# An attention and two expert layers in one kernel: the values' transfers issued as their buffer frees, shifted copies made head by head, the rests of q and k loaded by pairs of heads, and the first two batches of scores side by side

## The chip, the cores and the metric

The kernel runs on one core of a Trainium2 chip. The metric is the device time of one execution in microseconds (us), as the median of three runs.

## The reference

Only the first part, the attention, is touched by the change. What it feeds is told in one sentence each.

```python
def _attn_ref(q, k, v):
    B, H, S, D = q.shape          # 4, 8, 576, 64, float32
    window, dilation = 32, 4
    scores = np.matmul(q, k.transpose(0, 1, 3, 2)) / np.sqrt(D)
    rel = pos[:, None] - pos[None, :]
    mask_plain = (rel >= 0) & (rel < window)
    mask_dil = (rel >= 0) & (rel < window * dilation) & (rel % dilation == 0)
    # heads 0 to 3 use mask_plain, heads 4 to 7 mask_dil
    attn = softmax(np.where(mask, scores, -1e9))
    return np.matmul(attn, v)
```

The result, as 2304 rows of 512, goes through a soft mixture of experts (8 experts of 4 slots, weights moe_w1 and moe_w2, 33.5 MB in float32) and then through a second layer (h = x @ w_in, g = h - tanh(h), g @ w_out, weights of 64-bit elements, 16.8 MB), which gives the output of 2304 x 512.

## The kernel before

The attention is cut into 16 units. A unit is one head h of a pair of batch entries (`units`, each with h and the pair's number pr); the two entries lie on partitions 0 to 63 and 64 to 127 and are called ab or a in the code. Units 0 to 7 have the plain window ("nat" in the code), units 8 to 15 the dilated one. A unit has 9 blocks of 64 queries, and each block sees at most 96 keys. Four blocks at a time form a batch (`batches`, 38 of them; a dilated unit's last block counts twice). For each batch, TensorE (PE) makes scores (`scores`, tile sc, L401), DVE adds the mask and takes the maximum off (sm, L405 and L409), PE transposes (`flip`, tile pp, L420), ScalarE (ACT) takes the exponential (pT, L421), PE multiplies with the values (`mix`, tile pv, L431), and DVE divides (`norm`). The loop over k_ (from -2) does the scores of batch k_, the flip of batch k_ - 1 and the mix of batch k_ - 2, and between them takes up to three pieces off the list `extras` (`pick`). Such a piece is a `turn`: the transpose of a unit's q, k or rest on PE (tiles tr_q, tr_k, tr_e) and the copy to qT or kT on ACT.

q and k arrive in three tiles for a unit: "q" and "k" with the first 512 rows, and "e" with the rest, rows 512 to 575 of both. The transfers land in tiles that GpSimd (POOL) puts in another order (`regroup`, L279); unit 0's are loaded in that order at once. The values of a pair of units (two heads of the same pair of entries) go into one of two tiles vw, by turns: partitions 32 to 95 are filled by transfers (`load_v`), and partitions 0 to 31 hold the last 32 keys of the block before, copied from partitions 64 to 95 of the tile by POOL (`shift_v`, L301). For dilated units four more copies follow (L305), and a pair takes ten transfers instead of four. A tile of values is free when the mix of the last batch of the two units before has been done, which is what at stands for in the loop.

All transfers are issued by SyncE (SP), in program order; SP waits until the tile is free, and until one of eight semaphores in rotation is free, so at most eight are under way. Once an iteration one of the 24 first weight tiles of the experts is issued too (`w_load`, L229). In the first iterations PE also does matmuls whose result is not used (`stir`, tile warm; before them tile idle, L482). The vector phi is loaded in iteration 2 (L535) and scaled by POOL in iteration 3 (L538).

After the attention come the dispatch, the experts and the second layer. Their code is not changed. They run on the same engines, with a planner that fixes the second layer's order.

## Time and profile before

| | us |
|---|---|
| median of three runs (343.49 to 345.18) | 344.07 |
| the profiled execution | 346.59 |
| its span | 344.8 |
| PE busy | 309.5 |
| DVE busy | 223.5 |
| ACT busy | 163.8 |
| POOL busy | 108.6 |

The profile is of one execution, and all rows below are of it. PE's busy time holds matmuls at either of its two clocks. An engine's idle time matters where PE waits for it. The attention ends near 136 us of the span.

### The profile page before, as it was taken

The page shows a single profiled execution, that of the slowest core. Times are in us where ns is not written, and L with a number is a line of the kernel's source. Part 1 is how long each engine was busy: PE and PEld are TensorE (multiplying, and loading weights), DVE is VectorE, ACT ScalarE, POOL GpSimd, SP SyncE. Part 2 cuts the span into 40 slices and gives each one's busy share as a digit, 9 for nine tenths or more (in the row PEclk, how much of TensorE's full clock was granted, in tenths as well). Part 3 has the DMA queues.
Part 4 walks back from the last instruction along what each step waited for, and adds up shares of the span by engine and source line. Part 5 has one row for each costly group of instructions (what it writes and reads, how often), then busy time and mean ns, then how long its engine had stood idle before and what let it go on. Part 6 is the DMA issues. An engine that isn't in the chain of part 4 may idle for free.

```text
span 344.8 us, 7801 instructions
## 1 busy us (share of the span) xinstructions
PE 309.5 (90%) x2867; PEld 223.4 (65%) x2867; DVE 223.5 (65%) x744; ACT 163.8 (48%) x304; POOL 108.6 (31%) x195
## 2 busy tenths in 40 slices
PE   8977999988999998999999378879999999999990
PEld 5766887867788785643434256657765787787670
DVE  2355586773788686446315759868775678977591
ACT  2345455532373644322204367527784656655431
POOL 0354233205343110015003889966990000000000
PEclk9999699996999999999999789969999999999997
DMA  5877999596778898879999999573000013302003
GB/s 130 235 211 242 277 291 309 159 259 188 205 207 247 243 364 303 309 266 377 413 403 374 378 340 313 161 252 125 2 1 0 3 64 119 122 2 89 33 3 130
DMA packets 57885, 70.22 MB, mean 204 GB/s; under 512 B 29040, under 2 KB 45296, under 8 KB 57840
## 3 DMA queue, kind: packets, MB, share of 16 engines
q1 hardware_dynamic: 57840, 69.65, 62.7%
q8 instruction: 25, 0.41, 0.5%
q14 instruction: 20, 0.16, 0.2%
HBM read 64.91 MB, written 4.72 MB: 202 GB/s over the span
## 4 chain that ended last, share of the span: by engine, by line
PE 42%; POOL 7%; DVE 5%; issue 3%; ACT 2%; ACTq 0%; DVEq 0%; POOLq 0%
PE acc L1014 17%; PE h L1039 4%; PE h L1038 4%; PE hp L712 3%; PE sop L727 3%; POOL X L804 3%; PE ht L719 2%; DVE r L1050 2%; POOL X L801 1%; PE sp L634 1%; PE p L907 1%; PE msum L981 1%; ACT u L1043 1%; PE dt L607 1%; PE sit L626 1%
## 5 line engine op out<-in xcount | busy, mean ns | idle before, releaser
L1014 PE MATMUL acc<-whi,r 128*128 128x512 f32 x288 | 80.0, 398 | 1.8 <-DVE r L1050 1.1
L1043 ACT ACTIVATE u<-h,co 128x512 f32<-128x512 f32 (+1 forms) x80 | 51.0, 648 | 44.7 <-PE h L1039 36.8
L1050 DVE SCALAR_TENSOR_TENSOR r<-h,co,u 128x512 fp32r<-128x512 f32 (+1 forms) x80 | 55.0, 695 | 25.5 <-PE acc L1014 18.1
L1014 PEld LDWEIGHTS acc<-whi,r 128*128 128x128 f32 x288 | 52.5, 188 | 16.5 <-issue 2.4
L405 DVE CUSTOM_DVE_ANT_0 sm<-sc,m_sb 128x96 f32<-128x96 f32 x144 | 29.3, 259 | 11.4 <-PE sc L401 11.1
L401 PE MATMUL sc<-kT,qT 64*64 64x96 f32 (+1 forms) x608 | 35.8, 260 | 0.0
L431 PE MATMUL pv<-vw,pT 96*64 96x65 f32 x608 | 28.1, 234 | 6.9 <-POOL vw L301 4.3
L421 ACT ACTIVATE pT<-pp 96x512 f32<-96x512 f32 x38 | 23.1, 607 | 22.8 <-PE pp L420 22.8
L431 PEld LDWEIGHTS pv<-vw,pT 96*64 96x64 f32 x608 | 22.3, 143 | 15.2 <-issue 6.8
L1039 PE MATMUL h<-cT,Gs 128*128 128x512 f32 (+1 forms) x80 | 30.3, 385 | 0.9 <-DVE r L1050 0.7
L401 PEld LDWEIGHTS sc<-kT,qT 64*64 64x64 f32 x608 | 28.2, 139 | 4.3 <-issue 1.5
L339 ACT COPY qT<-tr_q 128x512 f32<-128x512 f32 x16 | 13.6, 848 | 25.8 <-PE tr_q L329 25.8
L420 PE MATMUL pp<-c_sb,sm 128*96 128x128 f32 x152 | 24.4, 285 | 0.0
L279 POOL TENSOR_SCALAR qm<-q 128x512 f32<-128x512 f32 x15 | 9.6, 641 | 42.3 <-PE tr_q L329 20.5
L409 DVE TENSOR_TENSOR sm<-sm,mx 128x384 f32<-128x384 f32 (+1 forms) x38 | 22.0, 580 | 1.2
L437 DVE TENSOR_SCALAR rd<-pv 128x4 f32<-128x4 f32 (+1 forms) x38 | 6.1, 159 | 25.4 <-PE pv L431 25.4
L301 POOL TENSOR_SCALAR vw<-vw 32x1024 f32<-32x1024 f32 (+1 forms) x16 | 13.2, 824 | 29.1 <-DMA vw<-in_v 27.4
L355 ACT COPY xT<-xt 128x512 f32<-128x512 f32 (+1 forms) x19 | 14.5, 784 | 12.4 <-PE xt L346 11.4
L1038 PE MATMUL h<-cT 128*128 128x512 f32 x64 | 20.2, 440 | 0.0
L1039 PEld LDWEIGHTS h<-cT,Gs 128*128 128x128 f32 x80 | 15.3, 191 | 5.7 <-DVE r L1050 2.2
L420 PEld LDWEIGHTS pp<-c_sb,sm 128*96 128x96 f32 x152 | 17.0, 130 | 3.0 <-issue 1.4
L804 POOL TENSOR_SCALAR X<-raw_i 128x512 bf16<-128x512 int16 x16 | 14.1, 908 | 11.4 <-DMA raw_i<-in_moe_w_in 10.9
(205 smaller groups left out, 524.1 us busy)
## 6 DMA issues: line engine op xcount, KB each, us to landing
w<-in_moe_w SPq DMA_DIRECT2D x60, 512.0 KB, 6.9
raw_o<-in_moe_w_out SPq DMA_DIRECT2D x16, 512.0 KB, 7.8
raw_i<-in_moe_w_in SPq DMA_DIRECT2D x15, 512.0 KB, 9.4
q<-in_q SPq DMA_DIRECT2D x15, 256.0 KB, 3.8
k<-in_k SPq DMA_DIRECT2D x15, 256.0 KB, 3.9
out<-X SPq DMA_DIRECT2D x14, 256.0 KB, 2.4
vw<-in_v SPq DMA_DIRECT2D x16, 144.0 KB, 3.6
vw<-in_v SPq DMA_DIRECT2D x32, 64.0 KB, 3.9
```

The costliest lines, as they stand in the source:

```text
L401: nc.tensor.matmul(dst[half, lo:hi], lhsT=qT[u % NQ][half, i:i + QB], rhs=keys[half], start=True, stop=True)
L405: nc.vector.tensor_tensor_reduce(out=sm[:, o:o + n, :].rearrange("p g k -> p (g k)"), in0=sc[:, o:o + n, :].rearrange("p g k -> p (g k)"), ...
L409: nc.vector.tensor_tensor(out=sm[:, o:o + n], in0=sm[:, o:o + n], in1=mx[:, o:o + n].unsqueeze(2).to_broadcast([128, n, KB]), op=ALU.subtract)
L420: nc.tensor.transpose(pp[:, i, :], sm[:, i, :], ident)
L421: nc.scalar.activation(out=pT, in_=pp, func=AF.Exp, scale=0.125)
L431: nc.tensor.matmul(pv[64 * ab:64 * ab + 64, i, :], lhsT=pT[:, o + x, 64 * ab:64 * ab + 64], rhs=w[:, ab, u % 2, j + x, :], start=x == 0, s ...
L804: nc.gpsimd.tensor_scalar(out=half(piece, 1, BF16), in0=quarter(piece, 3, I16), scalar1=2.0, scalar2=-2.0, op0=ALU.min, op1=ALU.max)
L1014: nc.tensor.matmul(live[key], lhsT=lhsT(), rhs=rhs(), start=new, stop=stop)
L1038: nc.tensor.matmul(live["h", key], lhsT=cT[:, 0:128], rhs=cT[:, c0:c0 + w], start=True, stop=True)
L1039: nc.tensor.matmul(live["h", key], lhsT=Gs[:, 128 * f:128 * (f + 1)], rhs=cT[:, c0:c0 + w], start=True, stop=True)
L1043: nc.scalar.activation(out=live["u", key], in_=live["h", key], func=AF.Square, scale=co[:, SC, f:f + 1])
L1050: nc.vector.scalar_tensor_tensor(out=live["r", key], in0=live["h", key], scalar=co[:, BB, f:f + 1], in1=live["u", key], op0=ALU.add, op1=A ...
```

## The change

- The values: `load_v` goes head by head, and within a head first batch entry 0, then 1; the rests come last. The transfers of units 2 and 3 are issued ahead of the loop; later pairs issue five transfers in each of two iterations, from the one in which the tile comes free, instead of three in each of four.
- The shifted copies: for the first pair ahead of the loop (before: in iterations 1 and 2); for later pairs head 0 in the third and head 1 in the fourth iteration after the tile comes free (before: both heads together, in the fifth at the latest).
- The rests "e" of q and k: one tile for two units, filled by four transfers, issued with the odd unit's turn. The first of them goes through ACT's queue.
- Unit 0's q and k: one transfer each, put in order by DVE.
- Iteration 0 stops after its scores and stirs, so that the scores of batches 0 and 1 follow each other; what was picked in it is picked in iteration 1.

```diff
@@ -251,47 +251,45 @@
             qT = [pools[i].tile([128, S], F32, name=f"qT{i}") for i in range(NQ)]
             kT = [pools[i].tile([128, 32 + S], F32, name=f"kT{i}") for i in range(NQ)]
             vw = [pools[i].tile([KB, 2, 2, NB + 1, D + 1], F32, name=f"vw{i}") for i in range(2)]
-            NR = 3
             raws, ms = {}, {}
 
-            def load_qk(u, nm):
+            def load_qk(u, nm, eng=nc.sync):
                 h, pr = units[u]
                 at = slice(2 * pr, 2 * pr + 2)
                 if nm == "e":
-                    t = raw.tile([128, 2, D], F32, tag=nm, name=f"{nm}_{u}", bufs=NR)
+                    t = raw.tile([128, 2, 2, D], F32, tag=nm, name=f"{nm}_{u}", bufs=2)
                     for x, src in enumerate((q, k)):
-                        nc.sync.dma_start(t[64 * x:64 * x + 64], src[at, h, 512:S].rearrange("a p d -> p a d"))
+                        for a in range(2):
+                            eng.dma_start(t[64 * x:64 * x + 64, :, a], src[2 * pr + a, h:h + 2, 512:S].rearrange("h p d -> p h d"))
+                    raws[u, nm], raws[u + 1, nm] = t[:, 0], t[:, 1]
                 else:
-                    src = q if nm == "q" else k
-                    if u == 0:
-                        t = raw.tile([128, 4, 2, D], F32, tag=nm + "m", name=f"{nm}m_{u}", bufs=2)
-                        for a in range(2):
-                            nc.sync.dma_start(t[:, :, a], src[2 * pr + a, h, 0:512].rearrange("(p r) d -> p r d", r=4))
-                        ms[u, nm] = t
-                        return
-                    t = raw.tile([128, 2, 4 * D], F32, tag=nm, name=f"{nm}_{u}", bufs=2)
-                    nc.sync.dma_start(t, src[at, h, 0:512].rearrange("a (p r) d -> p a (r d)", r=4))
-                raws[u, nm] = t
+                    t = raws[u, nm] = raw.tile([128, 2, 4 * D], F32, tag=nm, name=f"{nm}_{u}", bufs=2)
+                    eng.dma_start(t, (q if nm == "q" else k)[at, h, 0:512].rearrange("a (p r) d -> p a (r d)", r=4))
 
             def regroup(u, nm):
                 t = raws.pop((u, nm))
                 ms[u, nm] = raw.tile([128, 4, 2, D], F32, tag=nm + "m", name=f"{nm}m_{u}", bufs=2)
-                nc.gpsimd.tensor_scalar(out=ms[u, nm].rearrange("p r a d -> p a r d"), in0=t.rearrange("p a (r d) -> p a r d", r=4), scalar1=1.0, scalar2=0.0, op0=ALU.mult, op1=ALU.add)
+                dst, src = ms[u, nm].rearrange("p r a d -> p a r d"), t.rearrange("p a (r d) -> p a r d", r=4)
+                if u == 0:
+                    nc.vector.tensor_copy(dst, src)
+                else:
+                    nc.gpsimd.tensor_scalar(out=dst, in0=src, scalar1=1.0, scalar2=0.0, op0=ALU.mult, op1=ALU.add)
 
             def load_v(u):
                 h, pr = units[u]
                 w = vw[u // 2 % 2]
-                for ab in range(2):
-                    vb = v[2 * pr + ab, h:h + 2]
-                    if h < H // 2:
-                        for h2 in range(2):
-                            yield nc.sync.dma_start(w[32:96, ab, h2, 0:NB, 0:D], vb[h2].rearrange("(j p) d -> p j d", p=64))
-                        continue
-                    vi = vb.rearrange("h (i r) d -> h r i d", r=4)
-                    for h2 in range(2):
-                        for x in (1, 0):
-                            yield nc.sync.dma_start(w[32:96, ab, h2, 4 * x:4 * x + 4, 0:D], vi[h2, :, 64 * x:64 * (x + 1)].rearrange("r i d -> i r d"))
-                    yield nc.sync.dma_start(w[32:96, ab, :, 9, 0:D], vb[:, 512:576].rearrange("h p d -> p h d"))
+                nat = h < H // 2
+                for h2 in range(2):
+                    for ab in range(2):
+                        vb = v[2 * pr + ab, h + h2]
+                        if nat:
+                            yield nc.sync.dma_start(w[32:96, ab, h2, 0:NB, 0:D], vb.rearrange("(j p) d -> p j d", p=64))
+                            continue
+                        for x in range(2):
+                            yield nc.sync.dma_start(w[32:96, ab, h2, 4 * x:4 * x + 4, 0:D], vb[256 * x:256 * (x + 1)].rearrange("(i r) d -> i r d", r=4))
+                if not nat:
+                    for ab in range(2):
+                        yield nc.sync.dma_start(w[32:96, ab, :, 9, 0:D], v[2 * pr + ab, h:h + 2, 512:576].rearrange("h p d -> p h d"))
 
             def shift_v(u, parts=(0, 1)):
                 w = vw[u // 2 % 2]
@@ -299,7 +297,7 @@
                 for h2 in parts:
                     dst, src = (slice(1, NB), slice(0, NB - 1)) if nat else (slice(4, 8), slice(0, 4))
                     nc.gpsimd.tensor_scalar(out=w[0:32, :, h2, dst, 0:D], in0=w[64:96, :, h2, src, 0:D], scalar1=1.0, scalar2=0.0, op0=ALU.mult, op1=ALU.add)
-                if not nat:
+                if not nat and 1 in parts:
                     for r in range(4):
                         p = 32 * (r % 3)
                         nc.gpsimd.tensor_scalar(out=w[p:p + 32, :, :, 8 + r // 3, 0:D], in0=w[64:96, :, :, 4 + r, 0:D], scalar1=1.0, scalar2=0.0, op0=ALU.mult, op1=ALU.add)
@@ -468,10 +466,11 @@
                         regroup(u + 2, nm)
                         if u + 4 < NU:
                             load_qk(u + 4, nm)
-                    if nm == "e" and u + NR < NU:
-                        load_qk(u + NR, nm)
+                    if nm == "e" and u % 2 and u + 3 < NU:
+                        load_qk(u + 3, nm)
                 return done
 
+            load_qk(0, "e", nc.scalar)
             load_qk(0, "q")
             nc.sync.dma_start(c_sb[:, 0:128], cst[:, 0:128])
             load_qk(0, "k")
@@ -485,17 +484,21 @@
                     nc.vector.memset(kT[i][:, 0:32], 0.0)
                 nc.vector.memset(vw[i][:, :, :, :, D:D + 1], 1.0)
                 nc.vector.memset(vw[i][0:32, :, :, 0, 0:D], 0.0)
-            load_qk(0, "e")
-            for nm in "qke":
+            for nm in "qk":
+                regroup(0, nm)
+            for nm in "qk":
                 load_qk(1, nm)
-            for nm in "qk":
                 regroup(1, nm)
-            for _ in load_v(0):
-                pass
-            for nm in "qke":
-                load_qk(2, nm)
+            vloads = {u: load_v(u) for u in range(0, NU, 2)}
+            for u in (0, 2):
+                for _ in vloads[u]:
+                    pass
+                for nm in "qk" if u == 0 else "":
+                    load_qk(2, nm)
+            shift_v(0)
             for nm in "qk":
                 load_qk(3, nm)
+            load_qk(2, "e")
             warm = ps.tile([128, GB, D + 1], F32, tag="pv", name="warm").rearrange("p g d -> p (g d)")
 
             def stir(n):
@@ -503,10 +506,6 @@
                     nc.tensor.matmul(warm, lhsT=ident, rhs=m_sb[:, 0:GB * (D + 1)], start=True, stop=True)
 
             for k_ in range(-2, NBAT + 1):
-                if k_ == 1:
-                    shift_v(0, (0,))
-                if k_ == 2:
-                    shift_v(0, (1,))
                 if k_ >= 2 and len(w_sb) < min(WR, (k_ - 1) * WR // 31):
                     w_load(wright)
                 if k_ < 0:
@@ -519,6 +518,8 @@
                     scores(k_)
                 if k_ < 2:
                     stir(2)
+                if k_ == 0:
+                    continue
                 pick(k_)()
                 if k_ < 2:
                     stir(1)
@@ -548,15 +549,11 @@
                         w_load(early)
                 for u in range(2, NU, 2):
                     at = last[u - 3] + 2 if u > 2 else 0
-                    if k_ == at:
-                        vloads = load_v(u)
-                    if at <= k_ < at + 4:
-                        for _ in range(3):
-                            next(vloads, None)
-                    if k_ == min(at + 4, first[u] + 1):
-                        for _ in vloads:
+                    if at <= k_ < at + 2:
+                        for _, _ in zip(range(5), vloads[u]):
                             pass
-                        shift_v(u)
+                    if at + 2 <= k_ < at + 4:
+                        shift_v(u, (k_ - at - 2,))
             assert not extras
             mix(NBAT - 1)
             done0 = x_part(3, 1, 0)
```

Where this moves instructions. Names carry the unit's or the batch's number first (tr_q_1 is the transpose of unit 1's q, sc_1 the scores of batch 1). First PE from the scores of batch 0 to those of batch 2, before and now:

```order
L401 MATMUL sc_0_185<-kT0_101,qT0_99 64x96 x8
L503 MATMUL warm_153<-m_sb_92,c_sb_58 128x260 x2
L329 MATMUL tr_q_1_203<-c_sb_58,qm_1_134 128x128 x4
L503 MATMUL warm_153<-m_sb_92,c_sb_58 128x260
L329 MATMUL tr_k_1_214<-c_sb_58,km_1_136 128x128 x4
L317 MATMUL tr_e_1_224<-c_sb_58,e_1_131 128x128
L401 MATMUL sc_1_235<-kT0_101,qT0_99 64x96 x8
L503 MATMUL warm_153<-m_sb_92,c_sb_58 128x260 x3
L420 MATMUL pp_0_254<-c_sb_58,sm_0_186 96x128 x4
L401 MATMUL sc_2_263<-kT0_101,qT0_99 64x96 x2
```

```order
L399 MATMUL sc_0_191<-kT0_101,qT0_99 64x96 x8
L506 MATMUL warm_162<-m_sb_92,c_sb_58 128x260 x2
L399 MATMUL sc_1_209<-kT0_101,qT0_99 64x96 x8
L506 MATMUL warm_162<-m_sb_92,c_sb_58 128x260 x2
L327 MATMUL tr_q_1_227<-c_sb_58,qm_1_133 128x128 x4
L506 MATMUL warm_162<-m_sb_92,c_sb_58 128x260
L418 MATMUL pp_0_238<-c_sb_58,sm_0_192 96x128 x4
L327 MATMUL tr_k_1_245<-c_sb_58,km_1_137 128x128 x4
L315 MATMUL tr_e_1_255<-c_sb_58,e_0_105 128x128
L399 MATMUL sc_2_264<-kT0_101,qT0_99 64x96 x2
```

The scores of batch 1 have moved ahead of unit 1's three transposes, the flip of batch 0 has moved between them, and one stir is gone.

Second POOL from unit 3's regroups to unit 5's, before and now (vw0 holds the values of units 0 and 1, vw1 those of 2 and 3):

```order
L279 TENSOR_SCALAR qm_3_208<-q_3_149 128x2x4x64
L279 TENSOR_SCALAR km_3_219<-k_3_151 128x2x4x64
L301 TENSOR_SCALAR vw0_103<-vw0_103 32x2x8x64 x2
L279 TENSOR_SCALAR qm_4_284<-q_4_161 128x2x4x64
L279 TENSOR_SCALAR km_4_301<-k_4_171 128x2x4x64
L538 TENSOR_SCALAR phi_sb_59<-phi_sb_59 128x128
L279 TENSOR_SCALAR qm_5_390<-q_5_210 128x2x4x64
L279 TENSOR_SCALAR km_5_407<-k_5_221 128x2x4x64
L301 TENSOR_SCALAR vw1_104<-vw1_104 32x2x8x64 x2
```

```order
L276 TENSOR_SCALAR qm_3_232<-q_3_153 128x2x4x64
L276 TENSOR_SCALAR km_3_250<-k_3_155 128x2x4x64
L276 TENSOR_SCALAR qm_4_285<-q_4_170 128x2x4x64
L276 TENSOR_SCALAR km_4_302<-k_4_180 128x2x4x64
L299 TENSOR_SCALAR vw1_104<-vw1_104 32x2x8x64
L539 TENSOR_SCALAR phi_sb_59<-phi_sb_59 128x128
L299 TENSOR_SCALAR vw1_104<-vw1_104 32x2x8x64
L276 TENSOR_SCALAR qm_5_390<-q_5_234 128x2x4x64
```

Before, both heads of vw1 were shifted behind phi and unit 5's regroups. Now head 0 stands ahead of phi and head 1 right behind it; vw0's shift (not in these rows any more) now stands ahead of unit 2's regroups.

Third SP around the values of units 8 and 9 (vw0), before and now:

```order
L293 DMA vw0_103<-in_v 64x4x64 x3
L229 DMA w_10_1041<-in_moe_w1 128x1024
L293 DMA vw0_103<-in_v 64x4x64
L294 DMA vw0_103<-in_v 64x2x64
L293 DMA vw0_103<-in_v 64x4x64
L229 DMA w_11_1094<-in_moe_w1 128x1024
L273 DMA q_13_1119<-in_q 128x2x256
L273 DMA k_13_1136<-in_k 128x2x256
L263 DMA e_12_1155<-in_q 64x2x64
L263 DMA e_12_1155<-in_k 64x2x64
L293 DMA vw0_103<-in_v 64x4x64 x3
L229 DMA w_12_1163<-in_moe_w2 128x1024
```

```order
L267 DMA q_12_995<-in_q 128x2x256
L267 DMA k_12_1012<-in_k 128x2x256
L289 DMA vw0_103<-in_v 64x4x64 x5
L229 DMA w_10_1038<-in_moe_w1 128x1024
L289 DMA vw0_103<-in_v 64x4x64 x3
L292 DMA vw0_103<-in_v 64x2x64 x2
L229 DMA w_11_1093<-in_moe_w1 128x1024
L267 DMA q_13_1118<-in_q 128x2x256
```

The ten transfers of vw0 have only one weight between them now; before there were three weights, unit 13's q and k and unit 12's two rests. Before, the first five of these rows' transfers are entry 0's, and what unit 8's first four blocks read of entry 1 is the first of the last group of three; the tenth transfer comes behind one more weight.

## Rows read from the trace of the kernel before

**Rows 1.** Waits of PE from 0 to 136 us: total us, times, longest us.

```profile
PE pv L431 <- POOL vw L301: 4.3, 2, 2.3
PE pv L431 <- DMA vw<-in_v: 2.5, 1, 2.5
```

**Rows 2.** Timeline: start us, us, engine, instructions [idle before <- its end].

```profile
20.77 0.57 PE L431 MATMUL pv<-vw,pT 96*64 96x65 f32 x12 [2.26 <-POOL vw L301]
...
21.27 0.33 PE L317 MATMUL tr_e<-c_sb,e 128*128 128x128 f32 x1
```

**Rows 3.** Timeline around phi and the shift of unit 2.

```profile
22.50 0.62 POOL L279 TENSOR_SCALAR km<-k 128x512 f32<-128x512 f32 x1
...
26.64 0.59 SPq L535 DMA_DIRECT2D phi_sb<-in_moe_phi  x1
...
30.55 0.64 POOL L538 TENSOR_SCALAR phi_sb<-phi_sb 128x128 f32<-128x128 f32 x1 [7.42 <-DMA phi_sb<-in_moe_phi]
...
32.44 2.15 POOL L301 TENSOR_SCALAR vw<-vw 32x1024 f32<-32x1024 f32 x2
...
33.53 0.49 PE L431 MATMUL pv<-vw,pT 96*64 96x65 f32 x4 [2.02 <-POOL vw L301]
```

**Rows 4.** Timeline around the first values of unit 8.

```profile
65.03 2.51 SPq L293 DMA_DIRECT2D vw<-in_v  x3
...
73.19 1.90 SPq L293 DMA_DIRECT2D vw<-in_v  x3
...
78.45 1.13 PE L431 MATMUL pv<-vw,pT 96*64 96x65 f32 x14 [2.48 <-DMA vw<-in_v]
```

**Rows 5.** Stretches: busy us of PE, PEld, DVE, ACT, POOL; clock, DMA share, GB/s.

```profile
33.46:40.29 6.83, 6.76 (x57) 5.70 (x59) 2.64 (x16) 2.09 (x5) 2.26 (x4) 0.50 0.94 290
40.29:47.12 6.83, 6.83 (x115) 5.61 (x111) 5.73 (x35) 3.71 (x7) 3.32 (x4) 1.00 0.98 281
77.84:84.66 6.82, 6.21 (x53) 5.26 (x55) 2.12 (x12) 1.91 (x5) 4.38 (x8) 0.50 0.64 178
```

**Rows 6.** Timeline of the start.

```profile
9.34 0.88 PE L401 MATMUL sc<-kT,qT 64*64 64x96 f32 x16
...
12.64 1.12 ACT L339 COPY kT<-tr_k 128x512 f32<-128x512 f32 x1
...
13.96 1.58 PE L503 MATMUL warm<-m_sb,c_sb 128*128 128x260 f32 x6
...
15.91 0.88 PE L401 MATMUL sc<-kT,qT 64*64 64x96 f32 x16
...
16.02 0.59 ACT L421 ACTIVATE pT<-pp 96x512 f32<-96x512 f32 x1 [2.14 <-PE pp L420]
...
16.79 0.41 SPq L273 DMA_DIRECT2D k<-in_k  x1
```

**Rows 7.** The page's costliest groups and its DMA issues (last: us to landing).

```profile
L279 POOL TENSOR_SCALAR qm<-q 128x512 f32<-128x512 f32 x15 | 9.6, 641 | 42.3 <-PE tr_q L329 20.5
...
e<-in_q SPq DMA_DIRECT2D x16, 32.0 KB, 3.6
```

**Rows 8.** Long stretches, columns as in rows 5.

```profile
0.00:30.00 30.00, 25.89 (x265) 19.81 (x266) 13.59 (x79) 12.00 (x21) 7.59 (x15) 1.00 0.73 190
30.00:62.00 32.00, 29.86 (x402) 24.24 (x400) 20.82 (x118) 16.59 (x31) 13.35 (x18) 0.89 0.98 291
62.00:136.00 74.00, 71.15 (x1022) 56.60 (x1020) 52.36 (x283) 34.97 (x70) 19.72 (x41) 0.95 0.80 239
...
155.00:180.00 25.00, 24.42 (x213) 10.13 (x215) 10.00 (x24) 5.27 (x10) 6.09 (x12) 1.00 1.02 399
```

**Rows 9.** Timeline: the first shift for unit 4, its first product.

```profile
43.88 1.04 POOL L301 TENSOR_SCALAR vw<-vw 32x1024 f32<-32x1024 f32 x1 [0.89 <-DMA vw<-in_v]
...
49.34 0.69 PE L431 MATMUL pv<-vw,pT 96*64 96x65 f32 x16
```

## The prediction

> **What bounds the kernel now.** I read the waits of TensorE (PE) first. Up to 136 us, the end of the attention, it waits three times for any length, each time in front of the products with the values (pv): twice for GpSimd's shifted copies (4.3 us in two waits), once for the values' own transfer (2.5 us) [rows 1]. Everywhere else in this stretch the next matmul stands ready, so the attention lasts as long as PE's list plus these waits. The timeline gives their places: 18.5 to 20.77 us, 31.5 to 33.53 us and 75.97 to 78.45 us [rows 2 to 4].
>
> The timeline also names what is late each time. First: in program order GpSimd regroups units 1 to 3 before it shifts pair 0. Second: GpSimd's last regroup of unit 4 ended at 23.1 us; then the scaling of phi sat 7.42 us waiting for a transfer that SyncE (SP) issued only at 26.64 us, and the shift of unit 2, behind it, began at 32.44 us [rows 3]. Third: unit 8's first product needs head 0 of both batch entries. The second entry's is the seventh of ten value transfers, behind two weights, a q, a k and two rests; the ten start at 65.03 us, the seventh goes out at 73.19 us and lands some 5 us later [rows 4].
>
> Then the clock. Right behind the second and the third wait PE's granted clock is 0.50 (1.2 of 2.4 GHz) for 6.8 us each; behind the first it stays at 1.00 [rows 5, 8]. In the half stretch from 33.46 us PE issued 57 matmuls, in the equally long one behind it 115. DVE was busy 2.64 of the 6.83 us [rows 5], so PE's clock set that stretch.
>
> **The change part by part.**
>
> *First two batches together, unit 0 by regroup, shift of pair 0 ahead.* The scores of batch 1 (unit 0 alone) come right behind those of batch 0; unit 1's transposes follow. From the first scores at 9.34 us on, PE had no wait worth a sum until 18.5 us [rows 2, 6]. Now it does scores, two stirs, scores, two stirs. A stir is a third of 1.58 us, a batch of scores 0.88 us [rows 6] and a little less to the next start, so unit 1's q transpose starts near 12.9 us. ScalarE then has q's copy and k's copy (1.12 us each), the exponential between them (0.59 us) [rows 6] and two small copies, so unit 1's scores can start near 16.85 us. PE stands there near 15.1 us: a new wait of 1.75 us. Behind it, up to the transpose of unit 2's rest, stands the work that took 15.91 to 18.5 and 20.77 to 21.27 us before [rows 2, 6], 3.1 us, less the scores of unit 0 done ahead of the wait: 2.8 us. That transpose stands at 19.65 us instead of 21.27: 1.6 us won. The shift of pair 0 is out of the way: its values are SP's 7th to 10th issue, and only unit 1's regroups stand before it. What queues behind it on GpSimd, unit 2's regroups, is wanted near 17.5 us, two regroups of 0.64 us [rows 7] behind values that should land near 13.
>
> Two things take from this. The regroups of unit 0 on DVE do not occur before; the same shape costs 0.64 us on GpSimd, and a 128x512 copy out of PSUM 1.12 us [rows 6, 7]. I take 0.8, nearer the first since nothing comes from PSUM. q's hides behind the four idle matmuls; k's is late by perhaps 0.15 us, and k's copy, the scores and all else wait for it. And the rests of units 2 and 3 are now the last of 26 transfers, four of them issued by ScalarE; before, the 24th went out at 16.79 us, and a rest takes 3.6 us from issue to landing [rows 6, 7]: 20.4 us by that pace, some 0.8 us after PE wants it. Since SP has 22 to issue and not 26, I take 0.15 us of wait. Term: **1.3 us**, bounds 0.3 (late rest and k in full) and 2.7 (no new wait, a stir less).
>
> One page bears on the four transfers moved to ScalarE's queue. Before, all data came through one queue, at 190 GB/s in the first 30 us [rows 8]. The Trainium skill, "DMA: Bandwidth & Descriptors", section "Queues, rings and completion order", says that a DMA engine takes turns between the queues that have work for it; no run here shows two queues at once. By it unit 0's rests, 128 KB, would push in among the first q and k; the sum would then lose 0.7 us (see the rivals).
>
> *Shift of unit 2 in two parts, the first ahead of phi.* Its transfers now go out before those of unit 3's q and k, and ahead of the first head's shift stand the regroups of units 1 to 4, done at 23.1 us before [rows 3]. Half the shift takes 1.1 us; PE needs it near 30 us. The second head's still stands behind phi, but that head is first used two batches later, and phi is issued four issues sooner. Term: the wait of 2.02 us [rows 3] and the clock behind it. At half clock 57 matmuls took 6.83 us, at full 115 [rows 5]: 6.83 x (1 - 57/115) = 3.4; I take 3.3, as the mix differs. **5.3 us**; bounds of the clock's part 0 (it falls anyway) and 3.4.
>
> *Values of units 8 to 15: five and five transfers in two iterations, head by head.* What unit 8's first product needs is now the third of ten, not the seventh; the weights, q, k and rests go behind. From the first to the third takes under 2 us, where the seventh took 8 [rows 4]. Term: 2.48 us of wait, and the clock: from 77.84 us it was half for 6.82 us, with PE busy 6.21 of it [rows 5], half of which is 3.1. **5.6 us**.
>
> *Rests by pairs of heads.* Four transfers for two units, as before in number, and the first unit of a pair is loaded as far ahead as before. *Values of units 4 and 6* stand at nearly the same place of SP's list. Nothing for either; the cover is SP's lead (below for what it costs if that is gone).
>
> Sum: 1.3 + 5.3 + 5.6 = 12.2 us. The profiled execution, 346.59 us with a span of 344.8, would become 334.4; the median of the runs, 344.07, becomes **331.9 us**.
>
> Does it reach the end? Between 155 and 180 us PE runs almost without a gap (24.42 of 25 us) and transfers are busy 1.02 of the time [rows 8]. They are issued as PE frees tiles, so they move along if those ahead are done 12.2 us sooner. The DMA engines stood idle 27% of the first 30 us (8 us) and 20% of 62 to 136 us (15 us) [rows 8]. That is room enough; I pass the whole sum on.
>
> **The rivals.**
>
> *Transfers take the place of the copies.* Between 30 and 62 us they are busy 0.98 of the time [rows 8], and PE wants this data 6.6 us sooner (1.3 + 5.3). The tightest place is unit 4: its first shift was done at 44.9 us, its first product came at 49.34 us [rows 9], now wanted at 42.7. With SP not a bit earlier PE waits 2.2 us there, and the clock may fall behind it (3.3 us more). Against it: phi, which held GpSimd and through its regroups SP, comes about 4 us sooner, and the two transfers that are needed go first. 334 to 338 us, say 336.
>
> *The start loses its clock.* The new wait of 1.75 us plus a late rest might do what the one of 2.02 us did, although 2.26 us at 18.5 us did not: 3.3 us, giving 335.2.
>
> *Two queues take turns.* 128 KB at 190 GB/s [rows 8] put the first k 0.7 us later, and all behind it: 332.6 us. This is the mechanism of the page named above.
>
> *The gain stays in the attention.* If the transfers of the expert stage cannot start sooner, PE waits for weights near 150 to 180 us: 338 to 344 us. Against it the idle shares above.
>
> *Slower: half clock all along 30 to 62 us.* If PE, now ahead, waits for transfers at every unit, each wait may be followed by a half stretch as two were. PE was busy 29.86 us of these 32, 6.76 of them already at half [rows 5, 8]; the other 23 at half cost as much again: 355 us. It decides from some 12 us of such work on. Against it: only the values lie close, and a slowed PE lets the transfers catch up.
>
> **How the numbers follow.** Forecast 0.58; transfers 0.20; start's clock 0.08; two queues 0.06; gain kept back 0.05; slower 0.03. The forecast's own range goes from 330.4 (start at its upper bound) to 333.5. Eight in ten: 329.5 to 337 us; the lower end is upper bounds together and a little of the spread of runs, the upper takes in most of the transfers' case. Half a per cent, 1.7 us, is about what a measurement here can tell from no change. Faster: the first four and part of the fifth, 0.94; same 0.03; slower 0.03.
>
> **What would show it.** Right: PE's waits for the shifted copies and the values are gone from the list; the granted clock is 1.00 up to the end of the experts; a new wait of 1 to 2 us for ScalarE's copies near 15 to 17 us; the attention ends near 124 us. Wrong: a wait at pv for values or shift anew (units 4 or 8), a rest's transpose that waits over 1 us near 20 us, a half clock anywhere before 124 us, or an attention that ends at 124 us and a span that does not follow.

## The result and the profile after

The changed kernel takes 333.91 us (median of 4 runs, 331.91 to 334.58), the kernel before on the same chip 343.78 us (4 runs, 343.04 to 345.18): a ratio of 0.970 (95% interval 0.965 to 0.975), 9.9 us less. The prediction was 331.9 us with a range of 329.5 to 337.0; the time lies in it, 2.0 us above the forecast. The profiled execution took 333.81 us (span 332.0), where the sum had made 334.4 us of the one before; from one profiled execution to the other it is 12.8 us less.

The waits of TensorE (PE) in the attention of the changed kernel that the kernel before does not have, in total us, times, longest:

```profile
PE tr_e L315 <- ACT pT L419: 1.1, 1, 1.1
...
PE sc L399 <- ACT kT L337: 0.7, 1, 0.7
...
PE tr_k L327 <- DVE km L274: 0.4, 1, 0.4
```

Nothing waits at the products with the values (pv) any more, neither for GpSimd's shifted copies nor for the values [rows 1]. These three short waits of the start take their place. The long stretches of the changed kernel, with columns as in [rows 5]; the last line is the first half clock after the attention:

```profile
0.00:30.00 30.00, 26.31 (x282) 20.18 (x284) 16.12 (x85) 13.10 (x23) 11.58 (x20) 1.00 0.82 214
30.00:62.00 32.00, 31.86 (x479) 25.99 (x477) 24.87 (x139) 18.91 (x39) 11.88 (x16) 1.00 0.91 272
62.00:123.00 61.00, 60.81 (x923) 48.07 (x923) 46.42 (x255) 30.89 (x61) 18.00 (x38) 1.00 0.84 251
...
182.29:192.53 10.24, 8.43 (x52) 5.96 (x53) 6.76 (x14) 5.06 (x10) 9.07 (x17) 0.50 1.06 376
```

Against [rows 8], PE issues 479 matmuls from 30 to 62 us where it issued 402, and the granted clock there is 1.00 instead of 0.89. The end of the attention is seen in the first matmul behind it, that for mrow: first fence the kernel before, second fence the changed one.

```profile
134.78 0.49 PE L586 MATMUL mrow<-c_sb,mnl 128*128 128x128 f32 x2
```

```profile
122.70 0.49 PE L583 MATMUL mrow<-c_sb,mnl 128*128 128x128 f32 x2
```

In these two executions the attention is 12.1 us shorter, and from mrow to the end it is 209.3 us instead of 210.0. So what the attention gained arrives at the end. (The same rest took 207.1 to 211.5 us in the profiles of the experiments below, so single executions differ there by some us.) The three places of the prediction in the timeline of the changed kernel, the start first:

```profile
6.31 0.43 DVE L274 COPY km<-k 128x512 f32<-128x512 f32 x1 [2.24 <-DMA k<-in_k]
...
15.42 1.25 SPq L263 DMA_DIRECT2D e<-in_k  x2
...
16.12 0.71 PE L399 MATMUL sc<-kT,qT 64*64 64x96 f32 x12 [0.72 <-ACT kT L337]
...
18.41 0.66 ACT L419 ACTIVATE pT<-pp 96x512 f32<-96x512 f32 x1
...
19.97 0.30 PE L315 MATMUL tr_e<-c_sb,e 128*128 128x128 f32 x1 [1.05 <-ACT pT L419]
...
22.26 1.22 POOL L299 TENSOR_SCALAR vw<-vw 32x1024 f32<-32x1024 f32 x1
...
61.46 3.39 SPq L289 DMA_DIRECT2D vw<-in_v  x5
...
67.14 0.61 POOL L299 TENSOR_SCALAR vw<-vw 32x512 f32<-32x512 f32 x1 [4.44 <-DMA vw<-in_v]
...
69.16 0.69 PE L429 MATMUL pv<-vw,pT 96*64 96x65 f32 x16
```

The transpose of unit 2's rest (tr_e) stands at 19.97 us, 1.3 us ahead of [rows 2]. Its wait is put down to an exponential (pT) that had ended at 19.07 us, 0.9 us earlier; the last of the rest's transfers was issued from 15.42 us on, so it is probably the rest that is late. It is not late each time: in two kernels below that have the same code up to there ("The shift put back" and "The wait of the second stage filled") the same transpose stands without a wait at 19.53 and 19.32 us. The shift of unit 2's first head runs at 22.26 us, where both heads' ran from 32.44 us on [rows 3]. And unit 8's first five values go out at 61.46 us; the shift that waits for them ends at 67.75 us, 1.4 us before PE uses it at 69.16 us.

### The profile page after: what moved, and what is told of

The parts are those of the page before. It is cut to its first block, busy times and chain, and to the rows that moved or that the text cites. A ratio compares the mean times of both kernels' runs of the same rounds, so it can differ in the third digit from the quotient of the medians.

```text
span 332.0 us, 7818 instructions
## 1 busy us (share of the span) xinstructions
PE 304.3 (92%) x2865; PEld 218.6 (66%) x2865; DVE 225.8 (68%) x746; ACT 162.9 (49%) x304; POOL 108.3 (33%) x195
## 4 chain that ended last, share of the span: by engine, by line
PE 40%; DMA 9%; POOL 5%; DVE 4%; ACT 2%; issue 1%; ACTq 0%; DVEq 0%; POOLq 0%; SPq 0%
PE acc L1011 18%; DMA w<-in_moe_w 6%; PE h L1036 5%; PE h L1035 5%; DMA raw_o<-in_moe_w_out 3%; POOL X L801 2%; PE hp L709 2%; PE p L904 1%; PE sp L631 1%; DVE r L1047 1%; PE msum L978 1%; PE sop L724 1%; PE ht L716 1%; POOL X L798 1%; ACT u L1040 1%
## 5 line engine op out<-in xcount | busy, mean ns | idle before, releaser
L399 PE MATMUL sc<-kT,qT 64*64 64x96 f32 (+1 forms) x608 | 34.4, 252 | 0.7 <-ACT kT L337 0.7
L399 PEld LDWEIGHTS sc<-kT,qT 64*64 64x64 f32 x608 | 26.9, 133 | 5.1 <-issue 1.2
L429 PE MATMUL pv<-vw,pT 96*64 96x65 f32 x608 | 26.1, 227 | 0.1
L429 PEld LDWEIGHTS pv<-vw,pT 96*64 96x64 f32 x608 | 20.8, 137 | 7.7 <-issue 6.8
L407 DVE TENSOR_TENSOR sm<-sm,mx 128x384 f32<-128x384 f32 (+1 forms) x38 | 22.7, 597 | 1.2
L418 PE MATMUL pp<-c_sb,sm 128*96 128x128 f32 x152 | 23.5, 277 | 0.0
L1035 PE MATMUL h<-cT 128*128 128x512 f32 x64 | 21.0, 456 | 0.0
L418 PEld LDWEIGHTS pp<-c_sb,sm 128*96 128x96 f32 x152 | 16.2, 126 | 2.9 <-issue 1.4
L442 DVE TENSOR_TENSOR X<-pv,rd 128x256 f32<-128x256 f32 (+3 forms) x48 | 16.2, 356 | 1.3
```

Source lines behind the costliest of these rows:

```text
L399: nc.tensor.matmul(dst[half, lo:hi], lhsT=qT[u % NQ][half, i:i + QB], rhs=keys[half], start=True, stop=True)
L407: nc.vector.tensor_tensor(out=sm[:, o:o + n], in0=sm[:, o:o + n], in1=mx[:, o:o + n].unsqueeze(2).to_broadcast([128, n, KB]), op=ALU.subtract)
L418: nc.tensor.transpose(pp[:, i, :], sm[:, i, :], ident)
L429: nc.tensor.matmul(pv[64 * ab:64 * ab + 64, i, :], lhsT=pT[:, o + x, 64 * ab:64 * ab + 64], rhs=w[:, ab, u % 2, j + x, :], start=x == 0, s ...
L1035: nc.tensor.matmul(live["h", key], lhsT=cT[:, 0:128], rhs=cT[:, c0:c0 + w], start=True, stop=True)
```

## The experiments

Every ratio is to the kernel before on the same chip; the intervals are 95%. "One part alone" means the kernel before with that part.

### The shift of unit 2 alone

```
-                    if k_ == min(at + 4, first[u] + 1):
+                    if u == 2:
+                        if at + 2 <= k_ < at + 4:
+                            shift_v(u, (k_ - at - 2,))
+                    elif k_ == min(at + 4, first[u] + 1):
```

> The kernel before with one edit: the shift of unit 2 in two parts, the first ahead of phi's scaling; its four value transfers already stood ahead of phi. My theory (2.0 us of wait and 3.3 us of half clock): the wait before the products with unit 2's values is gone, no half clock at 33 to 40 us, the whole program 5.3 us faster. Rival 1, the clock falls there anyway: 2.0 us. Rival 2, phi or the values are the late ones and the shift only follows them: 0 to 1 us, with the wait still there. Rival 3, the gain is kept back further on, before the products of unit 4 or in the expert stage: the attention ends earlier by less than the wait taken away.

Measured: 345.48 us, ratio 1.005 (1.002 to 1.008). Not faster, if anything slower. Two rows of its timeline, SyncE's (SP) queue and PE, tell why:

```profile
74.25 1.90 SPq L293 DMA_DIRECT2D vw<-in_v  x3
...
77.82 1.13 PE L431 MATMUL pv<-vw,pT 96*64 96x65 f32 x14 [6.06 <-DMA vw<-in_v]
```

The wait at unit 2 is gone and the clock is 1.00 from 33.5 to 40.3 us, so PE reaches unit 8's products some 4 us sooner. But the seventh of unit 8's ten values goes out at 74.25 us, no sooner than before [rows 4], and PE waits 6.06 us for it instead of 2.48. So in this execution the transfers set the time up to unit 8. The term of 5.3 us is refuted as a term that stands alone; rival 3 of this run holds in substance, with unit 8 as the place.

### The order of the values alone

```
+                for h2 in range(2):
+                    for ab in range(2):
+                        vb = v[2 * pr + ab, h + h2]
+                        for x in range(2):
+                            yield nc.sync.dma_start(w[32:96, ab, h2, 4 * x:4 * x + 4, 0:D], ...)
...
+                    if u >= 8:
+                        if at <= k_ < at + 2:
+                            for _, _ in zip(range(5), vloads):
+                                pass
+                        if at + 2 <= k_ < at + 4:
+                            shift_v(u, (k_ - at - 2,))
+                        continue
```

> The kernel before with one edit: the values of units 8 to 15 issued head by head, five and five transfers in two iterations, and shifted head by head. My theory (2.5 us of wait and 3.1 us of half clock): the wait before unit 8's products is gone, the clock stays at 1.00 from 78 to 85 us, 5.6 us faster. Rival, the weights, q, k and rests that now go out later are wanted: the wait turns up at a transpose of units 9 or 10 and the gain is under 3 us.

Measured: 337.73 us, ratio 0.983 (0.980 to 0.987), 5.9 us by the medians. The attention's end (mrow) moves to 128.16 us. The wait at unit 8 is gone. At unit 2 PE waits 2.03 us as before, but the half stretch behind it lasts 3.42 us here and not 6.83. From 74 to 81 us:

```profile
74.00:81.00 7.00, 7.00 (x98) 5.90 (x96) 5.32 (x27) 4.33 (x11) 3.60 (x7) 1.00 0.89 258
```

### The start alone

```
+            load_qk(0, "e", nc.scalar)
+            load_qk(1, "e", nc.scalar)
             load_qk(0, "q")
...
+                if u == 0:
+                    nc.vector.tensor_copy(dst, src)
...
+            shift_v(0)
             for nm in "qk":
                 load_qk(3, nm)
...
+                if k_ == 0:
+                    continue
                 pick(k_)()
```

> The kernel before with the edits of the start alone: unit 0's q and k in one transfer each and regrouped by VectorE, the rests of units 0 and 1 through ScalarE's queue, scores of batches 0 and 1 together, the shift of pair 0 ahead of the regroups of units 2 and 3. My theory: the wait of 2.26 us at the first products with values goes, one or two waits near 15 to 20 us come (together 1.8 us in the changed kernel), and unit 2's rest is transposed 1.3 us sooner: 1.3 us faster, the waits at units 2 and 8 and their half clocks stay. Rival 1: the start alone moves the list against unit 2's late shift, which does not come sooner, so the gain ends in a longer wait there (3.3 us instead of 2.0) and the time does not change. Rival 2: the start gives 2.3 us, the whole wait.

Measured: 342.6 us, ratio 0.995 (0.992 to 0.999), 1.0 us by the medians. PE in its timeline:

```profile
18.83 0.33 PE L315 MATMUL tr_e<-c_sb,e 128*128 128x128 f32 x1
...
30.59 0.34 PE L429 MATMUL pv<-vw,pT 96*64 96x65 f32 x4 [1.53 <-POOL vw L299]
...
74.17 1.12 PE L429 MATMUL pv<-vw,pT 96*64 96x65 f32 x14 [4.16 <-DMA vw<-in_v]
```

The rest of unit 2 is transposed at 18.83 us with no wait, 2.4 us ahead of [rows 2], where rests are loaded unit by unit. PE reaches unit 8's products at 70.01 us, 6.0 us sooner than in the first profile, and 1.7 us of that goes in the longer wait (4.16 us instead of 2.48): a loss like that of rival 1, at another place and in part only. In this execution the attention ends at 130.78 us, 4.0 us sooner than in the first profile, while the medians show 1.0 us. How much of the lead the values take back in most executions stays open.

### The waits filled

```
                 pv = st["v", b] = ps.tile([128, GB, D + 1], F32, tag="pv", name=f"pv_{b}")
+                for _ in range({first[2]: 8, first[8]: 9}.get(b, 0)):
+                    nc.tensor.matmul(pv.rearrange("p g d -> p (g d)"), lhsT=ident, rhs=m_sb[:, 0:GB * (D + 1)], start=True, stop=True)
```

> The kernel before, with nothing taken away: 8 extra matmuls of 128x260 (0.26 us each, their result overwritten) ahead of the products with unit 2's first values and 9 ahead of those with unit 8's, so that TensorE works through the two waits of 2.02 and 2.48 us instead of standing. My theory, that the half clock follows from the standing still and its price is 3.3 and 3.1 us: the clock is 1.00 from 33 to 40 and from 78 to 85 us, the waits are replaced by the extra matmuls, and the program is 6.4 us faster although it does more. Rival, the half clock has another cause or its price lies in other engines: 0 us, or up to 1 us slower by the extra matmuls.

Measured: 345.33 us, ratio 1.005 (1.002 to 1.008). The experiment was mis-sized: the 8 matmuls took 3.67 us, not 2.1 us, as this row of PE shows (each counts twice), so PE was later than the wait would have made it. It says nothing on the price of the clock. Both filled places ran at 1.00; the only half stretch of the attention came behind the wait that was not filled, the 2.08 us at the first products (20.95 to 27.78 us).

```profile
34.10 3.67 PE L428 MATMUL pv<-m_sb,c_sb 128*128 128x260 f32 x16
```

Sized again, with the first wait filled too (`{0: 4, first[2]: 4, first[8]: 10}`):

> The kernel before with extra matmuls of 128x260 ahead of the products that wait, in number as in time that they take (0.46 us each at full clock): 4 before the first products of pair 0, 4 before those of unit 2, 10 before those of unit 8. Results are overwritten. TensorE then stands nowhere for 2 us up to 136 us. If its granted clock falls behind such a wait because it stood: 1.00 up to the end of the attention. What that is worth: up to unit 8 nothing, since the transfers set the time there; behind unit 8 the 3.1 us of the half clock from 77.84 us: 3 us faster than before, 2 to 3 us in the end of the attention. Rival, the half clock there costs nothing of its own: no change.

Measured: 342.77 us, ratio 0.997 (0.994 to 1.000). Two stretches, a row of PE, and the stretch behind it:

```profile
33.00:40.00 7.00, 7.00 (x108) 5.88 (x106) 4.59 (x26) 3.66 (x9) 3.59 (x6) 1.00 0.89 288
77.00:84.00 7.00, 6.98 (x98) 5.79 (x99) 4.45 (x23) 3.22 (x8) 4.87 (x10) 1.00 0.80 224
```

```profile
126.71 0.91 PE L433 MATMUL pv<-vw,pT 96*64 96x65 f32 x10 [1.51 <-DMA vw<-in_v]
```

```profile
127.00:134.00 7.00, 7.00 (x70) 5.26 (x70) 2.93 (x12) 2.59 (x3) 0.12 (x2) 0.54 0.55 188
```

With PE kept at work the clock is 1.00 in both places where it was 0.50 [rows 5], and the executions' mean clocks are 0.964 to 0.979, those of the kernel before 0.950 to 0.969. That fits the theory that the half clock followed the standing. Of the 3 us that I expected the medians show 1.2. PE is indeed 3.9 us ahead of the first profile shortly before unit 14 (the exponentials of the same batch stand at 122.82 and 126.74 us). But the old order of the values is late once more at this last pair: PE waits 1.51 us, a half stretch follows (126.62 to 133.45 us), and the attention ends at 134.39 us, 0.4 us sooner than in the first profile. A clock that is given back ahead of late values only makes the next wait, and here the next half stretch.

### The kernel before, profiled again

No edit.

> The kernel before, unchanged, profiled a second time: the first profiled execution took 346.59 us where the median of 29 runs is 343.62. If the sum of the prediction, 12.2 us, was right against that one execution and too large against the median because the half clock behind the waits is not granted alike in every execution, this profile has fewer or shorter half stretches before 136 us than 33.46 to 40.29 and 77.84 to 84.66, and the attention ends before 134.8 us. If it is the expert stage that differs, the attention ends there again and the stretch behind it is shorter than 210 us.

Measured: 345.68 us in that execution. Its waits of PE up to 136 us, then the stretches behind the waits at units 2 and 8, then PE at unit 14 and at the attention's end:

```profile
PE pv L431 <- POOL vw L301: 4.1, 2, 2.1
PE pv L431 <- DMA vw<-in_v: 2.3, 2, 1.4
```

```profile
33.57:40.40 6.83, 6.83 (x59) 5.75 (x61) 2.72 (x16) 2.09 (x5) 2.24 (x3) 0.51 0.87 276
77.56:84.40 6.84, 6.84 (x99) 5.79 (x101) 4.58 (x23) 3.37 (x9) 5.00 (x10) 1.00 0.78 227
```

```profile
126.49 0.56 PE L431 MATMUL pv<-vw,pT 96*64 96x65 f32 x10 [0.92 <-DMA vw<-in_v]
...
132.42 0.49 PE L586 MATMUL mrow<-c_sb,mnl 128*128 128x128 f32 x2
```

The same program has a half clock behind unit 2's wait again, but none behind unit 8's: the wait there is 1.42 us and not 2.48, another 0.92 us stand at unit 14, and the attention ends at 132.42 us, 2.4 us sooner than in the first profile. From there to the changed kernel's 122.70 us it is 9.7 us, near the 9.9 us that the medians differ by. But this execution as a whole is no shorter for it: from mrow to its end it takes 211.5 us instead of 210.0, with 13.65 us at half clock in the second stage (190.46 to 204.11 us) where the first profile has 6.83 us, and at 345.68 us it lies 1.8 us above the median too. So executions differ in where the half stretches fall; what the attention takes in a median one, two profiles do not show. Over 29 executions the kernel before took 341.85 to 348.07 us at mean granted clocks of 0.949 to 0.978, the faster rather at the higher clock (correlation of time and clock over the 29: -0.54).

### Values and shift together

The edits of the values above, and for unit 2:

```
+                    if u == 2:
+                        if k_ < 2:
+                            for _, _ in zip(range(3), vloads):
+                                pass
+                        if 2 <= k_ < 4:
+                            shift_v(u, (k_ - 2,))
+                        continue
```

> The kernel before with two edits together: the shift of unit 2 ahead of phi, and the values of units 8 to 15 head by head. Alone the first gave nothing (1.9 us slower by medians): PE came to unit 8's products 4.2 us sooner and waited 6.06 us there instead of 2.48, since the seventh of its ten values went out no sooner. Alone the second gave 5.9 us. My new theory, transfers set the time up to unit 8 in the kernel before and the new order of the values takes them off the path: with both, the shift's 4 to 5.3 us come in full, so 10 to 11 us faster than before, no wait before unit 8's products. The additive theory of the prediction, 5.3 and 5.6, says 10.9 us here and 5.3 for the shift alone, which is gone already. Rival, the shift is worth nothing at all wherever it is done: 5.9 us.

Measured: 336.63 us, ratio 0.981 (0.976 to 0.986), 7.3 us by the medians. The interval overlaps that of the values alone (0.980 to 0.987), and 10.9 us would be 0.968: neither the additive theory nor the one that put 4 to 5.3 us on the shift holds. The rival, 5.9 us (0.983), lies inside. In its profiled execution the first wait, at the shift of pair 0, was 3.37 us, and a half clock followed there (0.59 on average from 22.60 to 29.40 us); that execution took 341.17 us, 4.5 us more than the median, so the stretch need not be in the others.

### Values and start together

The diffs of these two parts above, in one kernel.

> The kernel before with the edits of the start and the new order of the values of units 8 to 15, without the earlier shift of unit 2 and without the rests by pairs. Alone the values gave 5.9 us and the start 1.0 us. By the sum of parts: 6.9 us, 337 us. Theory from the runs so far (transfers set the time up to unit 8's values unless these go out head by head; the shift's own place is worth nothing that the median shows, as the changed kernel with the shift behind phi took 333.25 us): the start's lead, lost at unit 8 when it stands alone, is kept here, so 9 to 10 us, about 334 us, with a wait of some 1.5 us at unit 2 that does not lower the clock. Rival, the rests by pairs or the place of unit 4's values carry a part: 335 to 336 us.

Measured: 334.92 us, ratio 0.974 (0.968 to 0.981), 8.0 us by the medians: 1.1 us more than the sum of the two alone, which would be 0.980 and so lies inside the interval, and 1.0 us short of the 9 to 10 that I expected. The attention ends at 124.67 us. PE at unit 2, and the stretch behind it:

```profile
31.98 0.34 PE L430 MATMUL pv<-vw,pT 96*64 96x65 f32 x4 [2.03 <-POOL vw L300]
```

```profile
31.98:38.80 6.82, 6.82 (x100) 5.80 (x102) 4.88 (x27) 3.80 (x8) 3.50 (x5) 1.00 1.03 326
```

The wait is as long as the one before (2.02 us, [rows 3]), and no half clock follows. That gives the price of the half stretch at this place. Two exponentials of ScalarE (ACT), of the same two batches, stand on either side of it; first the kernel before (first profile), then this one:

```profile
31.06 0.65 ACT L421 ACTIVATE pT<-pp 96x512 f32<-96x512 f32 x1
...
44.63 0.59 ACT L421 ACTIVATE pT<-pp 96x512 f32<-96x512 f32 x1 [0.57 <-PE pp L420]
```

```profile
29.52 0.65 ACT L420 ACTIVATE pT<-pp 96x512 f32<-96x512 f32 x1
...
40.08 0.59 ACT L420 ACTIVATE pT<-pp 96x512 f32<-96x512 f32 x1 [0.57 <-PE pp L419]
```

They are 13.57 us apart with the half stretch and 10.56 without, with the same wait between them: it costs 3.0 us.

### The shift put back behind phi in the changed kernel

```
+                    if u == 2:
+                        if k_ == 4:
+                            shift_v(u)
-                    if at + 2 <= k_ < at + 4:
+                    elif at + 2 <= k_ < at + 4:
                         shift_v(u, (k_ - at - 2,))
```

> The changed kernel with one part undone: the shift of unit 2 is done whole, behind phi's scaling and the regroups of unit 4 and one more pair, as before. In the kernel before that part alone gave nothing, because unit 8's values held the attention. Here nothing holds it behind unit 2. Theory, the shift's term is real once the values are out of the way: the wait before unit 2's products is back, 2 to 3 us, with a half clock behind it in some executions, and the program is 2 to 5.3 us slower than the changed kernel. Rival, phi is issued four issues sooner here and the shift behind it is done in time anyway: within 0.5 us of the changed kernel.

Measured: 333.25 us, ratio 0.972 (0.966 to 0.977) against 0.970 for the changed kernel: no difference that can be told. GpSimd (POOL) and PE in its timeline:

```profile
28.34 0.30 POOL L539 TENSOR_SCALAR phi_sb<-phi_sb 128x128 f32<-128x128 f32 x1 [5.36 <-DMA phi_sb<-in_moe_phi]
...
30.20 2.16 POOL L299 TENSOR_SCALAR vw<-vw 32x1024 f32<-32x1024 f32 x2
```

```profile
31.29 0.34 PE L429 MATMUL pv<-vw,pT 96*64 96x65 f32 x4 [1.52 <-POOL vw L299]
```

The wait is back with 1.52 us; the clock behind it is 1.00, and the attention ends at 123.99 us, 1.3 us later. That is what the place of the shift is worth in these two profiles, and the medians do not show it. Nor do the other executions look as if the clock fell: their mean clocks are 0.969 to 0.979, those of the changed kernel 0.970 to 0.976. The rival has the time right, though its reason, a shift that is done in time, does not hold.

### The rests of units 0 and 1 through SyncE

```
-            load_qk(0, "e", nc.scalar)
             load_qk(0, "q")
...
             for nm in "qk":
                 regroup(0, nm)
+            load_qk(0, "e")
```

> The changed kernel with the rests of units 0 and 1 issued by SyncE, behind k of unit 0 and the masks, and not by ScalarE ahead of all. By the rule that a DMA engine takes turns between queues: the first k lands sooner (4.55 us from issue to the regroup that waits for it in the changed kernel), its regroup and tr_k come 0.4 to 0.7 us sooner; but four issues of 0.6 us stand ahead of unit 1's q and k, 2.4 us later. If the first k is what sets the start: 0.4 to 0.7 us faster. If SyncE's issues set it (unit 1's regroups and the shift of pair 0): 0 to 1 us slower.

Measured: 335.9 us, ratio 0.978 (0.973 to 0.983), against 0.970 for the changed kernel: some 2 to 3 us slower, though the two intervals still touch. VectorE, then PE:

```profile
5.43 0.43 DVE L274 COPY km<-k 128x512 f32<-128x512 f32 x1 [1.51 <-DMA k<-in_k]
```

```profile
20.56 0.30 PE L315 MATMUL tr_e<-c_sb,e 128*128 128x128 f32 x1 [1.86 <-DMA e<-in_k]
...
44.59 0.57 PE L429 MATMUL pv<-vw,pT 96*64 96x65 f32 x12 [0.76 <-POOL vw L299]
```

The first k was regrouped at 5.43 us, 0.88 us sooner than the 6.31 us of the changed kernel, where ScalarE's queue runs beside SP's (6.15 to 6.52 us in its three variants below and above that keep this start). That agrees with the rule of the Trainium skill ("DMA: Bandwidth & Descriptors", section "Queues, rings and completion order") that the queues take turns. But its transpose came only 0.14 us sooner (6.65 against 6.79 us; 7.05 to 7.59 us in the three variants), and that does not reach the end: the rest of unit 2 makes PE wait 1.86 us instead of 1.05 or nothing, and the attention ends at 124.16 us instead of 122.70 (123.45 in the last experiment's kernel, which has the same attention). The 0.76 us at unit 4 cannot be put on this edit, since a kernel with the changed kernel's attention has them as well (0.89 us, in the last experiment). That the four issues on SP are the cause is likely by their place, but it rests on one profile.

### The rests of units 2 and 3 through ScalarE

```
-            load_qk(2, "e")
...
                     if k_ == -2:
                         pick(k_)()
+                    else:
+                        load_qk(2, "e", nc.scalar)
                     stir(2)
```

> The changed kernel with the rests of units 2 and 3 issued by ScalarE behind its copies of unit 0 (it stands idle there from 8.8 to 13.55 us), and not by SyncE behind q and k of unit 3. Theory, the wait of 1.05 us before the transpose of unit 2's rest is for that transfer, although the profile puts it down to the exponential that had ended 0.9 us earlier: the wait goes, but for what the copy of k still holds, 0.5 to 1.0 us faster than the changed kernel. Rival 1, it waits for the copy of q and the exponential as the profile says: no change. Rival 2, ScalarE's four issues of 0.65 us hold up its copy of unit 1's q: slower by up to 1 us. That SyncE is 2.5 us ahead may move later transfers too.

Measured: 335.62 us, ratio 0.976 (0.970 to 0.983); not faster than the changed kernel. PE:

```profile
19.00 0.33 PE L315 MATMUL tr_e<-c_sb,e 128*128 128x128 f32 x1
...
42.59 0.33 PE L429 MATMUL pv<-vw,pT 96*64 96x65 f32 x2 [0.28 <-DMA vw<-in_v]
43.81 0.57 PE L429 MATMUL pv<-vw,pT 96*64 96x65 f32 x12 [0.89 <-POOL vw L299]
```

The wait at tr_e is gone, and at unit 4 PE now waits 1.17 us in two rows for values and their shift. Neither can be put on this edit. The kernel of the next experiment, whose attention is the changed kernel's own, shows the same two things in its profile:

```profile
19.32 0.33 PE L315 MATMUL tr_e<-c_sb,e 128*128 128x128 f32 x1
...
43.90 0.57 PE L429 MATMUL pv<-vw,pT 96*64 96x65 f32 x12 [0.89 <-POOL vw L299]
```

So in some executions the rest is in time, and then PE, some 1 us sooner, waits at unit 4 instead. What the row of 1.05 us waited for is not settled by this run.

### The wait of the second stage filled

```
+                def stir(n):
+                    if f0 == 0:
+                        if "hw" not in live:
+                            live["hw"] = ps.tile([128, 512], F32, tag="h", name="h_warm", bufs=3)
+                        for _ in range(n):
+                            nc.tensor.matmul(live["hw"], lhsT=cT[:, 0:128], rhs=cT[:, 0:512], start=True, stop=True)
```

(called with 3 behind proj_a's products and with 10 behind proj_b's)

> The changed kernel with extra matmuls of 128x512 in the second stage, 3 behind the first batch's products with soT and 10 behind its second product, where TensorE stands 1.13 and 3.00 us (177.99 to 183.0 us) and its clock is half from 182.29 us on for 10.24 us. Their result is overwritten. Theory, the half clock there follows the standing and lies on the path (GpSimd waits 2.4 us at 194.75 us for a product that TensorE made at half clock): the clock stays at 1.00 until 213 us at least, and the program is 1.5 to 2.5 us faster than the changed kernel, about 332 us. Rival, the transfers and GpSimd's conversions set the pace there and the clock does not matter: no change. Rival, the extra matmuls delay the second batch: 0.5 us slower.

Measured: 333.11 us, ratio 0.970 (0.964 to 0.977), the same as the changed kernel. The stretch that ran at half clock there, and PE's wait further on:

```profile
182.29:192.53 10.24, 7.16 (x64) 5.19 (x62) 8.23 (x16) 5.96 (x13) 9.18 (x18) 1.00 1.06 378
```

```profile
200.16 0.64 PE L911 MATMUL p<-X,soT 128*32 128x256 f32 x8 [2.18 <-POOL co L946]
```

The clock is back at 1.00 there, and PE reaches the next products sooner, but then it stands 2.18 us for GpSimd's coefficients, where the changed kernel waited 1.26 us. The clock fell all the same later on, for 3.41 us from 201.59 us, so 1.00 until 213 us did not come. From mrow to the end this execution took 207.3 us instead of 209.3, but the kernel with the shift put back took 207.1 us there without any filling. Transfers are busy 1.06 of that stretch and GpSimd 9.18 of its 10.24 us, so they, and not PE's clock, are the likely pace there; that is argued, as no run took work from either.

## Why the prediction was right, and where it was not

**Direction, places and the end.** Right. In the profile the waits at pv are gone, the clock is 1.00 up to 182.29 us (the second stage's first product stands at 177.75 us), the attention ends near 123 us (124 forecast), and the rest of the program keeps its length, so the rival "the gain stays in the attention" did not occur. One of the signs of being wrong came as well: a rest's transpose that waits over 1 us near 20 us (1.05 us).

**The terms, from profile to profile.** How far PE is ahead can be read wherever both kernels do the same batch. Four exponentials serve as marks: ahead of unit 2's products and behind the half stretch there, then the same at unit 8. In the kernel before the first two stand at 31.06 and 44.63 us (rows under "Values and start together"), the other two here; in the changed kernel all four follow:

```profile
75.38 0.59 ACT L421 ACTIVATE pT<-pp 96x512 f32<-96x512 f32 x1
...
87.46 0.59 ACT L421 ACTIVATE pT<-pp 96x512 f32<-96x512 f32 x1
```

```profile
29.72 0.67 ACT L419 ACTIVATE pT<-pp 96x512 f32<-96x512 f32 x1
...
38.18 0.59 ACT L419 ACTIVATE pT<-pp 96x512 f32<-96x512 f32 x1 [0.57 <-PE pp L418]
...
68.89 0.59 ACT L419 ACTIVATE pT<-pp 96x512 f32<-96x512 f32 x1
...
75.39 0.59 ACT L419 ACTIVATE pT<-pp 96x512 f32<-96x512 f32 x1
```

The lead at these marks is 1.34, 6.45, 6.49 and 12.07 us: the start gave 1.3 us (1.3 in the sum), unit 2's place 5.1 (5.3), unit 8's 5.6 (5.6). So the sum accounts for all of the 12.1 us between these two executions, with nothing left over.

**Where the size was off: from one execution to the median.** The sum was made from an execution of 346.59 us and then taken in full from the median, 344.07 us, which is 2.5 us less. Profile against profile it is even 0.6 us too small (334.4 against 333.81 us); against the medians it is 2.3 us too large (12.2 against 9.9). The second profile shows one thing that the first has beyond others: the half stretch at unit 8 and 1.1 us of the wait there were not in it (0.92 us at unit 14 came in instead). But that execution is long as well, further on, so it is not shown that these are the 2 us that the forecast lacks.

**Start, 1.3 us.** The total is right (21.27 to 19.97 us), its parts are not: the wait for ScalarE's copy is 0.72 us and not 1.75, the regroup on VectorE 0.43 us and not 0.8, k costs 0.36 us and not 0.15. And the rest, which I had 0.15 us late, is 1.05 us late here and in time in two other executions of the same start.

**Rests by pairs, nothing.** Not refuted. The 1.05 us may be its price in this execution, but the transpose stands without a wait at 19.53 and 19.32 us in the two others, as it does at 18.83 us with rests unit by unit.

**Shift of unit 2, 5.3 us.** The size is right between the two profiles, the reason is not. Moving the shift is not what pays. Alone it gives nothing (the transfers up to unit 8 take it back), and with the values the intervals do not tell it from nothing. With the shift put back in the changed kernel, PE's lead still grows by 3.5 us at this place (29.32 and 39.38 us for the two exponentials): 1.52 us of wait come back, the half stretch does not. So most of the 5.1 us is the clock, and the clock holds there without the earlier shift too, with start and values alone as well. Why it does, no run shows.

**Values, 5.6 us.** Right in size: 5.9 us alone by the medians, 5.6 us between the two profiles. The row that carried it was right as well, but the mechanism is wider than I had it: the old order is late for unit 14 too (0.92 to 1.51 us in three profiles, once with a half stretch behind it), and it takes back what is gained ahead of unit 8, all of it with the shift alone and 1.7 of 6.0 us with the start alone. That start and values together give 8.0 us, and alone 1.0 and 5.9, fits this, but the interval does not exclude the plain sum.

**The clock's price, 3.3 and 3.1 us.** What the leads above leave beyond the waits of 2.02 and 2.48 us: 3.1 us at either place, and 3.0 us at unit 2 against the kernel with start and values. 3.3 was a little high.

**Rivals.** "Transfers take the place" did not come in the profile of the changed kernel, but the place was well chosen: in another execution of the same attention unit 4's products waited 0.89 us, and 0.76 and 1.17 us with the rests moved to other queues. No half clock followed. "Two queues": the first k is 0.88 us later, as that mechanism says, and its transpose 0.14 us. As a whole the second queue costs nothing that shows: without it the median is 2.0 us longer, though the intervals touch.

What stays open: why the clock holds at unit 2 in the kernels with the new start, which attention a median execution of the kernel before has, and what the rest of unit 2 waits for. No version ran that is faster than the changed kernel beyond the intervals.

## What to carry to other kernels

A wait that is removed is worth its length only if the next thing that the same engine needs is not paced by something slower: look for the latest place where a queue still sets the time, and begin the change there. Undo a part in the changed kernel as well as doing it alone in the old one, because parts that remove waits in a row need not add: the shift and the values alone are worth -1.9 and 5.9 us, and 7.3 together. And profile the kernel before twice ahead of a sum in single microseconds: a clock stretch that is in one execution need not be in the median.
